# One queue of transfers, issued by GpSimd in place of SyncE, in a decode-attention forward and backward

## The chip, the cores and the metric

The kernel runs on one core of one Trainium2 chip. The metric is the device time of one execution in microseconds (us). Three runs of the kernel before took 645.79, 646.20 and 646.21 us; their median is 646.2 us.

The engines are named as the profile names them: PE is TensorE (PEld its weight loads), DVE is VectorE, ACT is ScalarE, POOL is GpSimd and SP is SyncE. A trailing q (SPq, POOLq) is the sequencer of an engine, which also issues transfers. The transfers themselves run on 16 DMA engines that the core has.

## The reference

One decode step of attention over 32 heads with one query row each, forward and all gradients:

```python
B, H, Sq, Skv, Dh = 1, 32, 1, 8192, 128          # all bf16
scores = jnp.einsum('bhqd,bhkd->bhqk', q, k) * scale
attn = softmax(scores, axis=-1)
out = jnp.einsum('bhqk,bhkd->bhqd', attn, v)
out, vjp = jax.vjp(forward, q, k, v)
return out, *vjp(grad_out)                        # out, dq, dk, dv
```

For one head, k and v are 8192 x 128 bf16 values, 2 MB each. The kernel must read both once (128 MB over the heads, in units of 2^20 bytes) and write dk and dv, which are as large. With p the softmax row, dv is the outer product of p and grad_out; dp = v grad_out; ds = p (dp - sum(p dp)) scale; dk is the outer product of ds and q; dq = ds k.

## The kernel before, in words

**Tiles.** A head's k (or v, dk, dv) lies in SBUF as one tile of 128 partitions by 64 rows by 128 values: partition p holds 64 successive rows, so each partition's share is one contiguous piece of 16 KB in memory. `Kt` has three buffers (`K_BUFS`), `Vt` two (`V_BUFS`), and the result tiles `G_dk` and `G_dv` two each.

**Transfers.** `load_k` (L74) and `load_v` (L78) load a head's tile with one transfer of 2 MB; only head 0's k comes in four chunks of 512 KB. `outer` (L225) stores a finished result tile with one transfer of 2 MB, or two of 1 MB for heads 0 and 31. `q` is loaded at L81 and `out` and `dq` are stored at L258, 8 KB each. All of these are issued by SP, in program order, on one queue. The one transfer that SP does not issue is the load of `grad_out`, which ACT issues. An issue waits on its engine's queue until its buffer is free (loads) or its data is there (stores), and holds up the issues behind it.

**Order of work.** The program first lists the q and grad_out loads, then `load_k(0)`, `load_v(0)`, `load_k(1)`, `load_v(1)`; after these stands `make_identity`, two POOL instructions that write `ident` (masks.py:197 and masks.py:199). From `tc.manual_schedule()` on, each engine executes in the order that the program is written in. POOL has nothing to do after `ident`.

`ident` is an input of nearly all of the opening: DVE's `in_quad` (L99), the four transposes of q (L111), `lane` (L113), `ident_f` (L115), and through these `q_blk` (L117). Only after `q_blk`, in DVE's order, come the block transposes of head 0's k (`k_blocks`, L146), and then PE's scores (L157).

The loop body for head h computes the scores of k (L157), the softmax (L163 to L311), the transposes of v (L188, with ACT's copies at L179), out (L205), dp (L200), and the four quarters of dv (L215); interleaved with it are the previous head's dq (L205) and the four quarters of dk (L215). `load_k(h + 2)` stands after dk's second quarter and `load_v(h + 2)` after dv's third, except in head 0, where `load_k(2)` has a free buffer at once.

Of the kernel before, what the change touches and what calls it, by code (L numbers as in the profile page):

```python
# [23 lines left out]
def kernel(  # L24
# [11 lines left out]
    nc = tc.nc  # L36
# [23 lines left out]
    Kt, Vt, XK, XV, st = {}, {}, {}, {}, {}  # L60

    def rows_of(x, h, c, parts):
        L = NT // parts
        return x[0, h].rearrange("(p n) d -> p n d", p=P)[:, c * L:(c + 1) * L, :]

    def slots(X, c, parts):
        L = NT // parts
        return X[:, c * L:(c + 1) * L, :]

    def load_k(h):  # L70
        Kt[h] = kpool.tile([P, NT, D], BF16, tag="K", name="Kt")
        parts = NCH if h == 0 else 1
        for c in range(parts):
            nc.sync.dma_start(slots(Kt[h], c, parts), rows_of(k, h, c, parts))  # L74

    def load_v(h):
        Vt[h] = vpool.tile([P, NT, D], BF16, tag="V", name="Vt")
        nc.sync.dma_start(Vt[h][:], rows_of(v, h, 0, 1))  # L78

    rows = consts.tile([H, 2, D], BF16)  # L80
    nc.sync.dma_start(rows[:, 0, :], q.rearrange("b h s d -> (b h s) d"))  # L81
    nc.scalar.dma_start(rows[:, 1, :], grad_out.rearrange("b h s d -> (b h s) d"))
    load_k(0)
    load_v(0)
    load_k(1)
    load_v(1)

    ident = consts.tile([P, P], BF16)
# [119 lines left out]
    def outer(h, which, r):  # L208
        x = st[h]
        if r == 0:  # L210
            x[which] = gpool.tile([P, NT, D], BF16, tag=which, name="G_" + which)
        G, dst = x[which], out_2 if which == "dk" else out_3
        rep, row = x["ds"] if which == "dk" else x["p"], x["qd"][:, 0 if which == "dk" else 1, :]
        Q = NT // 4
        nc.vector.tensor_tensor(  # L215
            slots(G, r, 4).rearrange("p n (a b) -> p n a b", b=R),
            slots(rep, r, 4).unsqueeze(2).to_broadcast([P, Q, D // R, R]),
            row.rearrange("p (a b) -> p a b", b=R).unsqueeze(1).to_broadcast([P, Q, D // R, R]),
            op=ALU.mult)
        parts = 1  # L220
        if h == 0 or h == H - 1:
            parts = 2
        if r % (4 // parts) == 4 // parts - 1:
            c = r // (4 // parts)
            nc.sync.dma_start(rows_of(dst, h, c, parts), slots(G, c, parts))  # L225

    def rows_bc(h):
        x = st[h]
# [22 lines left out]
    def result(src, dst):  # L251
        half = small.tile([P, H], BF16, tag="half", name="half")
        nc.scalar.copy(half[:], src[:])
        fin_ps = psT.tile([P, CH, P], BF16, tag="T", name="fin_ps")
        nc.tensor.transpose(fin_ps[0:H, 0, :], half[:], ident[:])
        fin_sb = small.tile([H, D], BF16, tag="fin", name="fin_sb")
        nc.scalar.copy(fin_sb[:], fin_ps[0:H, 0, :])
        nc.sync.dma_start(dst.rearrange("b h s d -> (b h s) d"), fin_sb[:])  # L258

    for h in range(H + 1):  # L260
        p_ = h - 1
# [8 lines left out]
        if h > 0:  # L270
            ds_of(p_)
            outer(p_, "dk", 0)
            dq_of(p_, 0)
# [3 lines left out]
        if h > 0:  # L277
            dq_of(p_, 1)
            outer(p_, "dk", 1)
        if 0 < h and h + 2 < H:  # L280
            load_k(h + 2)
# [7 lines left out]
        if h > 0:  # L289
            outer(p_, "dk", 2)  # L290
# [36 lines left out]
        if 0 < h and h + 2 < H:  # L327
            load_v(h + 2)
# [3 lines left out]
        if h == H - 1:  # L332
            result(o_all, out_0)

    result(dq_all, out_1)
    order.__exit__(None, None, None)

# [29 lines left out]
```

## Time and profile before

| what | value |
|---|---|
| median of three runs | 646.2 us |
| span of the profiled execution, first to last instruction | 644.6 us |
| bytes read and written | 134.23 MB and 134.23 MB |
| DMA engines busy with the SP queue (q1) | 98.2% of the span |
| DVE, PE, ACT, POOL busy | 78%, 75%, 28%, 0% |
| POOL instructions | 6 |

The profile gives the profiled execution's own time as its span only; the median of the runs is 1.6 us more than that span, which is taken here as what lies around it. Busy shares are averages over stages with different limits, so a stage is read by its own stretch of the trace. "DMA share" in a table of stretches is the mean busy share of the 16 DMA engines, GB/s what all of them moved. Beside the views, the trace holds a record for each DMA packet; where durations of packets are given, they are medians of these records.

### The profile page before, as it was taken

Reading aid. Unit: us, or ns where it says so; the run is one execution under the profiler, and the core shown is the slowest. Engines: PE = TensorE matmul, PEld = TensorE weight load, DVE = VectorE, ACT = ScalarE, POOL = GpSimd, SP = SyncE. Lnnn points to the kernel's source line nnn. Section 1 sums busy time; section 2 is a strip of 40 time slices with the busy share of each in tenths; the row PEclk is TensorE's granted clock in tenths of the full one; section 3 lists DMA queues with packets and bytes.
Section 4 is the critical chain, followed back from the end, with each engine's and each line's share of the span. In section 5 each row is a group of like instructions: output and inputs, shape, how many; then the busy total and the mean of one; then the engine's idle time right before and its main releaser. Section 6 shows DMA issues by size and latency. Waiting matters only on the chain.

```text
span 644.6 us, 20935 instructions
## 1 busy us (share of the span) xinstructions
PE 482.0 (75%) x9673; PEld 443.9 (69%) x9673; DVE 505.9 (78%) x653; ACT 180.7 (28%) x332; POOL 0.7 (0%) x6
## 2 busy tenths in 40 slices
PE   3998898886777877768776787677876777877780
PEld 2887788785676766768666687567776676866670
DVE  5999899767977679867788777787767986778761
ACT  2333333322233231333222332123322233231230
POOL 0000000000000000000000000000000000000000
PEclk9666666665566655666556665566665566655665
DMA  8999999999999999999999999999999999999985
GB/s 350 404 428 429 424 427 424 428 429 421 418 429 428 428 425 430 430 426 431 425 428 428 430 426 428 428 428 427 427 429 431 424 432 424 430 426 429 427 362 244
DMA packets 19718, 269.80 MB, mean 419 GB/s; under 512 B 2352, under 2 KB 2352, under 8 KB 2864
## 3 DMA queue, kind: packets, MB, share of 16 engines
q1 hardware_dynamic: 19584, 268.47, 98.2%
q8 instruction: 75, 1.23, 0.7%
q14 instruction: 11, 0.09, 0.0%
q10 hardware_dynamic: 48, 0.01, 0.0%
HBM read 134.23 MB, written 134.23 MB: 416 GB/s over the span
## 4 chain that ended last, share of the span: by engine, by line
DMA 62%; PE 24%; DVE 9%; ACT 1%; issue 1%; SPq 0%; DVEq 0%; ACTq 0%
DMA Vt<-in_v_dram 61%; PE T_ps L188 15%; DVE XK_sb L146 4%; DVE G_dv L215 4%; PE m_ps L205 3%; PE dp_ps L200 2%; PE s_ps L157 2%; PE dp_ps L205 1%; DVE G_dk L215 1%; DMA Kt<-in_k_dram 1%; PE m_ps L300 1%; ACT p_rep L309 0%; PE s_ps L173 0%; ACT XT_sb L179 0%; PE m_ps L288 0%
## 5 line engine op out<-in xcount | busy, mean ns | idle before, releaser
L188 PE MATMUL T_ps<-ident_f,Vt 128*128 128x128 f32 x1024 | 217.0, 383 | 27.3 <-DMA Vt<-in_v_dram 24.7
L188 PEld LDWEIGHTS T_ps<-ident_f,Vt 128*128 128x128 f32 x1024 | 182.2, 206 | 45.2 <-PE m_ps L288 21.7
L215 DVE TENSOR_TENSOR G_dv<-p_rep,qd 128x2048 bf16<-128x2048 bf16 x128 | 148.2, 1220 | 60.9 <-DMA out_dram<-G_dv 52.8
L215 DVE TENSOR_TENSOR G_dk<-ds_rep,qd 128x2048 bf16<-128x2048 bf16 x128 | 155.6, 1218 | 4.6 <-DMA out_dram<-G_dk 3.6
L146 DVE STREAM_TRANSPOSE XK_sb<-Kt 128x1024 f32<-128x1024 f32 x128 | 148.3, 1214 | 5.8 <-DMA Kt<-in_k_dram 3.2
L179 ACT COPY XT_sb<-T_ps 128x1024 f32<-128x1024 f32 x128 | 128.7, 1008 | 83.9 <-PE T_ps L188 77.2
L157 PE MATMUL s_ps<-q_blk,XK_sb 128*128 128x4 bf16 x2048 | 59.8, 168 | 94.6 <-DVE pdt L239 87.6
L157 PEld LDWEIGHTS <-XK_sb 128*128 128x128 bf16 x2048 | 57.1, 104 | 103.9 <-DVE pdt L239 96.6
L200 PE MATMUL dp_ps<-do_blk,XT_sb 128*128 128x2 bf16 x2048 | 67.0, 164 | 18.0 <-ACT XT_sb L179 17.6
L200 PEld LDWEIGHTS <-XT_sb 128*128 128x128 bf16 x2048 | 65.5, 103 | 20.7 <-ACT XT_sb L179 20.2
L205 PE MATMUL dp_ps<-ds_rep,Kt 128*128 128x1 bf16 x2048 | 64.0, 165 | 0.4 <-DVE ds_rep L241 0.4
L205 PEld LDWEIGHTS <-Kt 128*128 128x128 bf16 x2048 | 59.5, 104 | 5.7 <-issue 5.6
L249 ACT COPY dq_all<-dp_ps 128x1 f32<-128x1 f32 x32 | 5.1, 159 | 205.2 <-PE dp_ps L205 182.8
L205 PEld LDWEIGHTS <-Vt 128*128 128x128 bf16 x2048 | 57.0, 96 | 0.7
L205 PE MATMUL m_ps<-p_rep,Vt 128*128 128x1 bf16 x2048 | 56.5, 163 | 0.0
L309 ACT ACTIVATE p_rep<-e,rinv 128x256 bf16<-128x256 f32 x32 | 16.3, 508 | 64.6 <-DVE rinv L307 64.6
L307 DVE RECIPROCAL rinv<-m_ps 128x1 f32<-128x1 f32 x32 | 5.4, 168 | 35.2 <-PE m_ps L300 35.1
L234 ACT CAST qd<-s_ps 128x256 bf16<-128x256 f32 x32 | 11.9, 372 | 32.5 <-PE s_ps L230 32.5
L299 ACT ACTIVATE e<-s_ps,nbias 128x64 f32<-128x64 f32 x32 | 10.1, 314 | 32.5 <-DVE nbias L295 32.5
L241 DVE SCALAR_TENSOR_TENSOR ds_rep<-dp_ps,pdt,p_s 128x256 bf16<-128x256 f32 x32 | 15.5, 484 | 4.6 <-PE dp_ps L200 1.3
L163 DVE TENSOR_TENSOR sm<-s_ps,in_quad 128x256 f32<-128x256 f32 x32 | 13.6, 425 | 6.0 <-PE s_ps L157 2.0
L300 PEld LDWEIGHTS m_ps<-rs,ones_f 128*128 128x128 f32 x64 | 17.6, 334 | 0.0
(44 smaller groups left out, 153.1 us busy)
## 6 DMA issues: line engine op xcount, KB each, us to landing
Vt<-in_v_dram SPq DMA_DIRECT2D x32, 2048.0 KB, 30.1
Kt<-in_k_dram SPq DMA_DIRECT2D x31, 2048.0 KB, 30.3
out_dram<-G_dv SPq DMA_DIRECT2D x30, 2048.0 KB, 34.5
out_dram<-G_dk SPq DMA_DIRECT2D x30, 2048.0 KB, 33.7
out_dram<-G_dv SPq DMA_DIRECT2D x4, 1024.0 KB, 14.4
out_dram<-G_dk SPq DMA_DIRECT2D x4, 1024.0 KB, 13.2
Kt<-in_k_dram SPq DMA_DIRECT2D x4, 512.0 KB, 5.1
out_dram<-fin_sb SPq DMA_DIRECT2D x2, 8.0 KB, 12.8
```

What stands on the lines that cost most here:

```text
L146: nc.vector.transpose(XK[h][:, :, :, u, :], slots(Kt[h], u, NCH).rearrange("p g d -> p (g d)").bitcast(F32).rearrange("p (g w j) -> p g w ...
L157: nc.tensor.matmul(out[:, g, :], lhsT=cols[:, g, c // 2, c % 2], rhs=q_blk[:, h, c, :], start=(c == 0), stop=(c == 2 * NB - 1), skip_group ...
L163: nc.vector.tensor_tensor(x["sm"][:], x["s"][:, 0:NT].rearrange("p (a g) -> p a g", a=NQ).unsqueeze(2) .to_broadcast([P, NQ, NCH, CH]), in ...
L179: nc.scalar.copy(X[:], st[h].pop("T")[:])
L188: nc.tensor.transpose(T_ps[:, i, :], words[:, m * P:(m + 1) * P], ident_f[:])
L200: nc.tensor.matmul(st[h]["dp"][:, n:n + 2], lhsT=X[:, i, e2, :], rhs=do_blk[:, h, e2, :], start=(e2 == 0), stop=(e2 == 1), skip_group_chec ...
L205: nc.tensor.matmul(out_col, lhsT=Xt[:, n, :], rhs=rep[:, n, 0:1], start=(n == 0), stop=(n == NT - 1), skip_group_check=True)
L215: nc.vector.tensor_tensor(slots(G, r, 4).rearrange("p n (a b) -> p n a b", b=R), slots(rep, r, 4).unsqueeze(2).to_broadcast([P, Q, D // R, ...
L234: nc.scalar.copy(x["qd"][:].rearrange("p a d -> p (a d)"), x["s"][:, 256:512])
L241: nc.vector.scalar_tensor_tensor(out=x["ds"][:], in0=x["dp"][:, 0:NT].unsqueeze(2).to_broadcast([P, NT, R]), scalar=pdt[:], in1=x["p_s"][: ...
L300: nc.tensor.matmul(x["m"][:, 0:1], lhsT=ones_f[:], rhs=rs[:], start=True, stop=True, skip_group_check=True)
L309: nc.scalar.activation(x["p"][:], e[:].unsqueeze(2).to_broadcast([P, NT, R]), ACT.Copy, scale=rinv[:])
```

## The change

All transfers that SP issued are issued by POOL. The order in which they are written, their sizes and the number of queues stay. ACT still issues the load of grad_out. Five issue sites change, which give 138 transfers: 35 loads of k (four of them the chunks of head 0), 32 loads of v, 68 stores of dk and dv, and three of 8 KB (q, out, dq).

```diff
@@ def load_k(h):
-            nc.sync.dma_start(slots(Kt[h], c, parts), rows_of(k, h, c, parts))
+            nc.gpsimd.dma_start(slots(Kt[h], c, parts), rows_of(k, h, c, parts))
@@ def load_v(h):
-        nc.sync.dma_start(Vt[h][:], rows_of(v, h, 0, 1))
+        nc.gpsimd.dma_start(Vt[h][:], rows_of(v, h, 0, 1))
@@ load of q
-    nc.sync.dma_start(rows[:, 0, :], q.rearrange("b h s d -> (b h s) d"))
+    nc.gpsimd.dma_start(rows[:, 0, :], q.rearrange("b h s d -> (b h s) d"))
     nc.scalar.dma_start(rows[:, 1, :], grad_out.rearrange("b h s d -> (b h s) d"))
     load_k(0)
     load_v(0)
@@ def outer(h, which, r):
-            nc.sync.dma_start(rows_of(dst, h, c, parts), slots(G, c, parts))
+            nc.gpsimd.dma_start(rows_of(dst, h, c, parts), slots(G, c, parts))
@@ def result(src, dst):
-        nc.sync.dma_start(dst.rearrange("b h s d -> (b h s) d"), fin_sb[:])
+        nc.gpsimd.dma_start(dst.rearrange("b h s d -> (b h s) d"), fin_sb[:])
```

## The prediction

> **What bounds the kernel now.** I read the page first, then stretches of the trace, the opening in order of time, and the issues with their times to landing. From the page come the transfer load, the queue's share and the chain that ended last:
>
> ```profile
> DMA  8999999999999999999999999999999999999985
> GB/s 350 404 428 429 424 427 424 428 429 421 418 429 428 428 425 430 430 426 431 425 428 428 430 426 428 428 428 427 427 429 431 424 432 424 430 426 429 427 362 244
> ...
> q1 hardware_dynamic: 19584, 268.47, 98.2%
> ...
> DMA 62%; PE 24%; DVE 9%; ACT 1%; issue 1%; SPq 0%; DVEq 0%; ACTq 0%
> ...
> Vt<-in_v_dram SPq DMA_DIRECT2D x32, 2048.0 KB, 30.1
> Kt<-in_k_dram SPq DMA_DIRECT2D x31, 2048.0 KB, 30.3
> ```
>
> All slices but the first and the last stand at 9, and the chain is 62% transfer. A load of 2 MB takes 2.097 MB / 427 GB/s = 4.9 us of the 16 DMA engines, but lands 30.3 us after its issue: some 25 us of other transfers stand ahead of it. SP issues far ahead of need, so a later issue is free until it eats those 25 us.
>
> The stretches show how level the middle is and what the end looks like (columns: busy time of PE, PEld, DVE, ACT, POOL, granted clock, DMA share, GB/s):
>
> ```profile
> 100.00:560.00 460.00, 349.23 (x6962) 320.81 (x6961) 362.85 (x463) 129.71 (x233) 0.00 (x0) 0.59 1.01 427
> ...
> 632.00:634.00 2.00, 0.00 (x0) 0.00 (x0) 0.00 (x0) 0.00 (x0) 0.00 (x0) 0.50 0.96 401
> 634.00:636.00 2.00, 0.00 (x0) 0.00 (x0) 0.00 (x0) 0.00 (x0) 0.00 (x0) 0.50 0.58 241
> ...
> 638.00:640.00 2.00, 0.00 (x0) 0.00 (x0) 0.00 (x0) 0.00 (x0) 0.00 (x0) 0.50 0.57 242
> ```
>
> In the middle no DMA engine idles. At the end 0.57 of 16, that is nine engines, still work for 6 us and more after the other seven are done. The nine late ones set the end.
>
> How far compute could run without transfers is in the chain in order of time (start, us, what):
>
> ```profile
> 17.09 4.63 DVE G_dv L215 x4
> ...
> 84.34 4.63 DVE G_dv L215 x4
> ...
> 135.42 1.94 PE T_ps L188 x8
> ...
> 614.30 1.94 PE T_ps L188 x8
> ```
>
> Four heads take 84.34 - 17.09 = 67.3 us while compute leads: 16.8 us each. Once transfers lead, 24 heads take 614.30 - 135.42 = 478.9 us: 19.95 us each. The margin is 3.1 us per head.
>
> **The change part by part.** It adds and removes no byte; 138 issues leave SP and go to POOL, which has only six instructions (0.7 us busy). Nothing is queued on SP after them. Five costs follow, (a) being the price of one issue.
>
> *(a) One issue.* SP's rows give 0.33 us for a store and 0.39 to 0.46 us at the opening. POOL issues nothing in this trace. Bounds: below, SP's 0.33 us; above, 1.5 us, the whole of the smallest transfer (q, 8 KB, from issue to landing), since making a list of 128 rows should not exceed making one of 32, moving it and reporting it. I take 1.1 us, which is q's 1.5 us less its 0.39 us of issue: POOL must do in instructions what a unit does for SP, so I lean to the upper row.
>
> *(b) The first transfer.* The opening, in order of time:
>
> ```profile
> 0.73 0.20 POOL masks.py:197 MEMSET ident<- 128x128 bf16 x1 [0.29 <-POOLq L351]
> 0.74 0.39 SPq L81 DMA_DIRECT2D rows<-in_q_dram  x1
> ...
> 1.01 0.29 POOL masks.py:199 TENSOR_SCALAR_AFFINE_SELECT ident<-ident 128x128 bf16<-128x128 bf16 x1
> 1.19 1.84 SPq L74 DMA_DIRECT2D Kt<-in_k_dram  x4
> ...
> 3.26 0.86 DVE L117 TENSOR_TENSOR q_blk<-tp_q,in_quad 128x128 bf16<-128x128 bf16 x4
> ...
> 7.85 2.47 DVE L146 STREAM_TRANSPOSE XK_sb<-Kt 128x1024 f32<-128x1024 f32 x2 [0.40 <-DMA Kt<-in_k_dram]
> ```
>
> q's issue and the first of four K chunks end at 1.19 + 1.84/4 = 1.6 us; packets follow. With two POOL issues from 0.73 us it is 0.73 + 2 x 1.1 = 2.9 us: +1.3 us. Nothing covers that, since from here on the DMA engines never idle. The other three chunks come 1.1 us apart and each needs 0.524 MB / 427 GB/s = 1.23 us, so they keep up. At 0.33 us per issue the term is -0.2 us; at 1.5 us it is +2.1 us, plus 3 x 0.27 us for the chunks, +2.9 us.
>
> *(c) `ident` behind the loads.* In program order eight issues (q, four chunks, v0, k1, v1) stand ahead of `make_identity` on POOL. `ident` is ready at 0.73 + 8 x 1.1 + 0.5 = 10.0 us, not 1.3. Behind it are `in_quad` 0.29, `four` 0.62, transposes 0.6, `q_blk` 0.86 and four block transposes of 1.23 each: 17.3 us in place of 10.3, so compute is 7 us late. The cover is what the queue holds:
>
> ```profile
> Kt<-in_k_dram SPq DMA_DIRECT2D x1, 2048.0 KB, 26.3
> ...
> out_dram<-G_dv SPq DMA_DIRECT2D x1, 1024.0 KB, 14.3
> ```
>
> The first line is k2, issued at 4.79 us: it lands at 31.1 us. The second is head 0's first dv half, issued at 19.48 us, far before that. After the change it would be ready at 19.48 + 7 = 26.5, issued by 27.6, against a queue that drains at 31.1 + 1.3 = 32.4 us: hidden by 4.8 us. The second half (21.8 + 7 + 1.1 = 29.9 against 34.9) and v2 (23.4 + 7 + 1.1 = 31.5 against 37.3) are hidden too. At 1.5 us per issue compute is 10.2 us late, the first half is issued by 31.2 against 34.0 us: still hidden. Cost zero; if the cover were gone, each us beyond it would cost one. Slack per head then returns the 7 us, 3.1 us at a time.
>
> *(d) The other 130 issues.* Each is up to 0.8 us longer, hidden behind 25 us of queue. In the tail, the last dk half is issued after 630.4 us and the late engines run until 643 us; that half is 8 packets of 0.31 us (packet records) on each engine, 2.5 us, so 10 us of slack hide 2 x 1.1 us. Zero.
>
> *(e) The packets.* The records show per DMA engine 611 ns for 16 KB, 309 ns for 8 KB, 159 ns for 4 KB, and one packet of 4 bytes, 9 ns, that closes each transfer. If POOL's lists have the same packets the cost is zero. One more closing packet per transfer would be 138 x 9 ns = 1.2 us. Below zero nothing is likely: the 16 KB packet already runs 26.8 GB/s in every slice. I take half of it, 0.6 us.
>
> Sum: +1.3 + 0 + 0 + 0.6 = +1.9 us on a span of 644.6 us; with the 1.6 us around it, 648.1 us. The median before is 646.2 us. A difference under 0.2% (1.3 us) is about what a measurement of this kernel cannot tell from none.
>
> Two rules stand against the rows. DVE is busy 78% of the span, its longest runs being four G_dv products and four block transposes, 4.63 + 4.5 = 9.2 us; the 25 us of queue cover even a list that waits for all of that. The Trainium skill's page "SBUF — State Buffer" (the note on DVE blocking a DMA issued from GpSimd) says that GpSimd can't write its descriptors while certain VectorE instructions hold the shared port pair, and advises SyncE or ScalarE; no row here shows POOL issuing. By it alone, with the queue as cover, the sum does not change. The page "DMA: Bandwidth & Descriptors", Specifications, gives about 1 us to the first byte for a GpSimd transfer and 0.6 us from SyncE. As an estimate worked out from that page, (b) would be 0.4 us in place of 1.3, and the whole 647.2 us.
>
> **The rivals.**
>
> *Transfers run slower.* POOL's lists could cut the 16 KB rows, or load some engines more than others. For it: 15,744 packets of 16 KB make up nearly all the time, and nothing here shows POOL's packets. Against it: sizes in the code are unchanged. Cut at 8 KB: 15,744/16 x (2 x 309 - 611) ns = 984 x 7 ns = 6.9 us, so 655 us; at 4 KB, 984 x 25 ns = 24.6 us, 673 us.
>
> *DVE is held up by POOL's writing.* It decides from 3.1/4 = 0.78 us of DVE time lost per issue, four issues a head. At 0.9 us, 0.12 x 4 x 32 = 15 us: 663 us. For it: compute would become the bound with only 16% to spare. Against it: DVE has idle time before its G_dv products (60.9 us in all) that takes up part.
>
> *Nothing shows.* An issue costs 0.6 us or less, or `ident` is written first: 646 to 647 us. For it: SP's issue is 0.33 us and the queue hides almost everything.
>
> *Faster.* The nine late engines run over 6 us longer than the seven. If POOL's lists share rows out so that this is evened, the nine give up 7/16 of some 7 us to 9 us of lag: 3 to 4 us, 643 to 644 us. For it: the seven are idle at the end. Against it: all transfers have 128 rows, a multiple of 16, so a share other than eight each has no reason.
>
> **How the numbers follow.** Chances: the forecast's case 47, of which 13 lie within 0.2% (under 647.5 us); slower transfers 20; DVE held up 6; nothing shows 17, of which 2 end below -0.2%; faster 10. Slower 34 + 20 + 6 = 60, same 13 + 15 = 28, faster 12. The likeliest case alone spans 646.0 us (-0.2 in (b), 0 in (e)) to 650.3 us (+2.9 and +1.2). The range goes down to 644.0, the dearer half of the faster case, and up to 661.0, past the 8 KB cut (655 us) and a third of the way on to the 4 KB cut (673 us); it leaves out about 5 below and 13 above.
>
> **What would show it.** (a) SPq's issue rows turn into POOLq rows; the gap between successive chunks at the opening gives the price. (b) First K data moves from about 2.2 to 3.5 us. (c) `in_quad` starts near 10 us, L146 ends near 17 us, and the DMA share stays at 9 from 20 to 45 us; a dip there would be cover that failed. (d) Loads still land about 30 us after issue. (e) 19,584 packets in the data queue and 427 GB/s in the middle; more packets, or fewer GB/s, mean the slower-transfer rival. If heads stay 19.95 us apart, only the opening counts; DVE's mean time of 1.22 us for G_dv rising above 1.3 us would mean that DVE is held. The prediction is wrong if an issue on POOL takes several us, or if the middle's rate moves at all: 1% of it is 6 us.

## The result and the profile after

The changed kernel takes 648.05 us (median of five runs, 647.40 to 648.86) against 646.15 us for the kernel before beside it: a ratio of 1.0032, with a 95% interval of 1.0019 to 1.0044. The forecast was 648.1 us, slower. That the number was met so closely is luck: the two terms that it put above zero were both too large, and another one, of 1.0 us, was missing.

The page of the changed kernel, with the lines that answer to those of before:

```profile
DMA  8999999999999999999999999999999999999985
GB/s 321 409 425 430 422 424 426 428 425 428 430 428 426 429 428 427 427 427 431 428 424 429 432 423 432 426 430 421 425 432 424 429 429 427 423 430 427 426 359 228
...
q0 software_dynamic: 19536, 268.47, 97.9%
...
Vt<-in_v_dram POOLq DMA_DIRECT2D x32, 2048.0 KB, 29.4
Kt<-in_k_dram POOLq DMA_DIRECT2D x31, 2048.0 KB, 29.9
```

The same bytes move on another queue at the same rate. Loads still land 29 to 30 us after their issue, so POOL too issues some 25 us ahead. The middle, in the same stretch as before (columns as there; POOL is the fifth, 49.86 us):

```profile
100.00:560.00 460.00, 350.96 (x6980) 322.94 (x6978) 364.81 (x466) 129.78 (x236) 49.86 (x94) 0.59 1.01 427
```

427 GB/s at a DMA share of 1.01, as before. Where, then, are the 1.7 us of span (646.3 less 644.6)? The opening, in order of time:

```profile
1.28 0.64 POOL L81 DMA_DIRECT2D rows<-in_q_dram  x1 [0.83 <-POOLq L351]
1.91 2.13 POOL L74 DMA_DIRECT2D Kt<-in_k_dram  x4
...
5.59 0.22 POOL masks.py:197 MEMSET ident<- 128x128 bf16 x1
5.74 0.53 POOL L74 DMA_DIRECT2D Kt<-in_k_dram  x1
6.36 0.30 POOL masks.py:199 TENSOR_SCALAR_AFFINE_SELECT ident<-ident 128x128 bf16<-128x128 bf16 x1
...
8.63 4.60 DVE L146 STREAM_TRANSPOSE XK_sb<-Kt 128x1024 f32<-128x1024 f32 x4
```

One issue takes 0.53 us on POOL (the first, q's, 0.64), and q's starts at 1.28 us, where SP's stood at 0.74. By the packet records the first packet of k starts at 3.17 us instead of 2.22. `ident` is complete at 6.7 us, and L146 ends at 13.2 instead of 10.3 us.

The end shows in SP's waits at the last line of the program, first in the kernel before and then in the changed kernel (waiting line, what it waits for, us in total, times, longest):

```profile
SPq L362 <- PEq L362: 0.6, 2, 0.4
```

```profile
SPq L362 <- PEq L362: 1.6, 2, 1.2
```

SP waits 1.0 us longer for the other engines after its last transfer has landed. The instructions of that line say for whom (changed kernel; durations min/median/max in ns, first and last start in us):

```profile
L362 POOLq DRAIN  x3: 46/87/13567, 632.0 to 646.0; - x3
L362 SPq DRAIN  x3: 7/7/7, 644.5 to 645.8; - x3
```

POOL's long drain starts at 632.0 us, behind its last issue, and ends at 632.0 + 13.57 = 645.6 us. SP had passed its own waits at 644.5. In the kernel before, no POOL drain is longer than 0.39 us:

```profile
L362 POOLq DRAIN  x3: 34/78/389, 1.0 to 644.3; - x3
```

With the packet records the span splits without a rest. "Stretch" runs from the first to the last data packet, "end" from there to the last instruction:

| kernel | first data packet | stretch | end | span |
|---|---|---|---|---|
| before | 2.22 | 640.82 | 1.57 | 644.6 |
| changed | 3.17 | 640.54 | 2.57 | 646.3 |
| difference | +0.95 | -0.28 | +1.00 | +1.7 |

These are two single executions. The medians differ by 1.9 us, which is what the first packet and the end add up to (0.95 + 1.00). The -0.28 of the stretch is less than executions of one kernel differ by: the eleven of the run with the tail on SP, for example, have spans from 644.5 to 646.1 us. The end too varies by itself: it is 1.4 to 1.9 us in the kernel before and in the six runs below in which POOL does not finish last.

### The profile page after: what moved, and what is told of

It reads as the page before. It is cut to its first block, busy times and chain, and to the rows that moved or that the text cites. A ratio compares the mean times of both kernels' runs of the same rounds, so it can differ in the third digit from the quotient of the medians.

```text
span 646.3 us, 20936 instructions
## 1 busy us (share of the span) xinstructions
PE 481.8 (75%) x9673; PEld 444.0 (69%) x9673; DVE 505.4 (78%) x653; ACT 180.4 (28%) x332; POOL 73.9 (11%) x144
## 4 chain that ended last, share of the span: by engine, by line
issue 69%; DMA 14%; POOL 9%; DVE 4%; PE 1%; POOLq 0%; ACT 0%; DVEq 0%; ACTq 0%
DMA Kt<-in_k_dram 9%; DMA Vt<-in_v_dram 5%; POOL out_dram L225 4%; POOL Kt L74 2%; DVE XK_sb L146 2%; POOL Vt L78 2%; PE s_ps L157 1%; DVE G_dv L215 1%; DVE G_dk L215 1%; PE T_ps L188 0%; DVE sm L163 0%; POOLq L225 0%; DVE q_blk L117 0%; POOL rows L81 0%; DVE mx L284 0%
## 5 line engine op out<-in xcount | busy, mean ns | idle before, releaser
L215 DVE TENSOR_TENSOR G_dv<-p_rep,qd 128x2048 bf16<-128x2048 bf16 x128 | 148.2, 1221 | 59.2 <-DMA out_dram<-G_dv 48.7
L146 DVE STREAM_TRANSPOSE XK_sb<-Kt 128x1024 f32<-128x1024 f32 x128 | 147.9, 1213 | 4.7 <-DMA Kt<-in_k_dram 2.0
L74 POOL DMA_DIRECT2D Kt<-in_k_dram x35 | 18.6, 533 | 219.2 <-PE dp_ps L205 219.2
L78 POOL DMA_DIRECT2D Vt<-in_v_dram x32 | 17.0, 532 | 215.5 <-PE m_ps L320 215.5
L225 POOL DMA_DIRECT2D out_dram<-G_dk x34 | 18.1, 532 | 84.8 <-DVE G_dk L215 65.6
L225 POOL DMA_DIRECT2D out_dram<-G_dv x34 | 18.1, 532 | 36.5 <-DVE G_dv L215 31.5
## 6 DMA issues: line engine op xcount, KB each, us to landing
out_dram<-G_dv POOLq DMA_DIRECT2D x4, 1024.0 KB, 13.2
```

Source lines behind the costliest of these rows:

```text
L74: nc.gpsimd.dma_start(slots(Kt[h], c, parts), rows_of(k, h, c, parts))
L78: nc.gpsimd.dma_start(Vt[h][:], rows_of(v, h, 0, 1))
L146: nc.vector.transpose(XK[h][:, :, :, u, :], slots(Kt[h], u, NCH).rearrange("p g d -> p (g d)").bitcast(F32).rearrange("p (g w j) -> p g w ...
L215: nc.vector.tensor_tensor(slots(G, r, 4).rearrange("p n (a b) -> p n a b", b=R), slots(rep, r, 4).unsqueeze(2).to_broadcast([P, Q, D // R, ...
L225: nc.gpsimd.dma_start(rows_of(dst, h, c, parts), slots(G, c, parts))
```

## The experiments

Theory A: the cost sits at the two ends, 0.95 us before the first packet and 1.0 us in POOL's drain, and the middle is free. Theory B: `ident` behind the loads, which made compute 2.9 us late, is the cost. Theory C: POOL's issues or packets cost a little each in the middle. Spans and packets below come from one profiled execution of a run, times are medians with the ratio to the kernel before on the same chip. The kernel before is at 645.8 to 646.0 us on those chips, so sums that start from 646.15 us can be 0.2 to 0.4 us high.

### Opening back on SP

```diff
+ (nc.sync if h <= 2 else nc.gpsimd).dma_start(... k ...)
+ (nc.sync if h <= 1 else nc.gpsimd).dma_start(... v ...)
+ nc.sync.dma_start(... q ...)
```

> Only the opening goes back to SP: q, k0 (four chunks), v0, k1, v1 and k2; the other 128 transfers stay on POOL, ident is written at once. Theory A (the ends: a first packet 0.95 us later and a drain of POOL's list that ends about 1.0 us after SP's own waits would; the middle is free): span 646.3 - 0.95 = 645.3 us, time 647.1 us, and POOL's last drain still ends some 1.9 us after the last data packet. Theory B (ident behind the loads, which made compute 2.9 us late, is the whole cost): span 644.6 us, time 646.2 us. Theory C (the middle: POOL's issues or packets cost a little each): span 646.3 us, time 648.0 us.

Measured 647.41 us (1.0022, 1.0006 to 1.0037), span 645.9. The first data packet is back at 2.21 us and the end stays long at 2.27 us, as A says, and B is refuted: with `ident` written at once the time does not return to that of the kernel before. (Its interval, 646.3 to 648.3 us, holds both A's and C's time.) But the stretch is 641.44 us, 0.9 longer than in the changed kernel, which A does not explain. The packet records say where it is: this execution's data packets took 633.2 us per DMA engine, against 631.7 in the changed kernel and in the kernel before. (The run had 129 transfers on POOL, not 128.)

### Tail back on SP

```diff
+ (nc.sync if h == H - 1 else nc.gpsimd).dma_start(... dk, dv ...)
+ nc.sync.dma_start(... out, dq ...)
```

> Only the tail goes back to SP: head 31's stores of dv and dk and the two 8 KB stores; the opening and the middle stay on POOL. Theory A: POOL's drain is over before the last data lands, so span 646.3 - 1.0 = 645.3 us, time 647.05 us, with the first data packet still at 3.2 us. Theory B and theory C: span 646.3 us, time 648.0 us.

Measured 647.05 us (1.0019, 1.0010 to 1.0028), span 644.8. First data packet 3.17, end 1.41 us. A's time exactly; the interval (646.6 to 647.8 us) leaves out B's and C's 648.0. The drain is off the path when POOL's last transfers land before SP's:

```profile
L362 POOLq DRAIN  x3: 46/103/23625, 615.7 to 644.5; - x3
L362 SPq DRAIN  x3: 7/7/7, 644.0 to 644.3; - x3
```

It ends at 615.7 + 23.6 = 639.3 us, and SP is ready only at 644.0.

### Opening and tail back on SP

> Opening and tail both go back to SP, the 122 transfers between stay on POOL. Theory A: span 644.3 to 644.6 us, time 646.0 to 646.2 us, as before the change. Theory B: the same 644.6 us (the opening alone does it, as in the run with the opening on SP). Theory C: span 646.2 us or more, time 647.9 us.

Measured 646.90 us (1.0015, 1.0006 to 1.0024). Both ends are as in the kernel before (2.23 and 1.42 us), but the stretch is 642.44 us and the median 0.8 us above A. The two ends are confirmed, and the middle is not quite free here, although it was in the run with the tail alone (stretch 640.25 us). The profiled execution was the slowest of the eleven. Its packets took 633.0 us per engine, which is 1.3 of the 1.6 us that its stretch is above the kernel before. What lifts the median is not shown by one trace.

### `ident` first

```diff
+ ident = consts.tile([P, P], BF16)
+ make_identity(nc, ident[:])
  rows = consts.tile([H, 2, D], BF16)
  nc.gpsimd.dma_start(... q ...)
```

> All on POOL as in the change, but the two instructions that write ident stand ahead of the first k chunk on POOL. Compute is ready some 3 us sooner, the first k packet 0.3 to 0.5 us later. Theory A: span 646.6 to 646.8 us, time 648.3 to 648.5 us, although compute starts earlier. Theory B: span 644.9 us, time 646.5 us. Theory C: span 646.3 us, time 648.0 us.

Measured 648.29 us (1.0045, 1.0032 to 1.0058), span 646.5. L146 ends at 11.6 instead of 13.2 us, so compute starts 1.6 us sooner, and the first data packet comes at 3.54 us, 0.37 later. The span follows the packet (+0.2 us), not the compute. This is A against B in one run: making POOL's useful work earlier made nothing faster, since it put two instructions ahead of the first load. The times of this run and the changed kernel's overlap; the verdict rests on the order of events, not on their difference.

### Opening alone, and tail alone, on POOL

The same two parts from the other side, on the kernel before.

> The kernel before, with only the opening moved to POOL: q, k0 (four chunks), v0, k1, v1, k2; the other 128 transfers stay on SP. Theory A (two ends, middle free): first data packet at 3.2 us in place of 2.2; time from the last data packet to the end as before, 1.6 us; span 644.6 + 0.95 = 645.6 us, time 647.1 us. Theory B (late ident is the whole cost): span 646.3 us, time 648.0 us. Theory C (a little per transfer in the middle): span 644.6 to 644.8 us, time 646.2 us.

Measured 647.11 us (1.0024, 1.0015 to 1.0033) against A's 647.1; first data packet 3.15 us, stretch 640.06 us. It is 1.26 us above the kernel before, a little more than the 0.93 us by which the packet is later. This run matters for a rival that the first three leave open: by their times alone, a middle that costs 1 us on POOL, with ends that cost less, would do as well. Here the middle is on SP, and the opening alone costs its full price. The changed kernel's own stretch, no longer than before, says the same.

> The kernel before, with only the tail moved to POOL: head 31's stores of dv and dk and the two 8 KB stores. Theory A: first data packet at 2.2 us, and the end comes 2.3 to 2.6 us after the last data packet in place of 1.6; span 645.5 us, time 647.0 us. If that drain grows with the number of transfers that POOL has issued (6 here, 138 in the change), it stays at 1.6 us and the span at 644.6 us. Theory B and C: span 644.6 us, time 646.2 us.

Measured 646.26 us (1.0007, 0.9999 to 1.0016), first data packet 2.22, end 1.82 us, and SP's last wait 0.6 us as before. With six transfers on POOL the drain (630.7 + 12.75 = 643.4 us) is over before SP's own waits are (643.6). So the drain is not a fixed price; the expectation's second case holds. Two more runs went to what sets it.

### What the drain grows with

```diff
+ (nc.gpsimd if h >= 16 else nc.sync).dma_start(... k, v, dk, dv ...)   # tail on POOL; h >= 7 in the second run
```

> The second half of all heads on POOL, with the tail: about 68 transfers on POOL, opening and first half on SP. If POOL's last drain takes longer the more transfers POOL has issued (SP's last wait for the other engines was 0.6 us with 6 transfers on POOL, 1.2 with 129, 1.6 with 138): that wait 0.8 to 1.0 us, span 644.9 us, time 646.5 us. If the count does not matter: 0.6 us, 644.6 us, 646.1 us, or 1.6 us, 645.6 us, 647.1 us. Rival D as above adds 0.8 us to any of these.

> Heads 7 to 31 and the tail on POOL, the first seven heads on SP: 104 transfers on POOL, fewer than the 138 of the change. Theory E (POOL's last drain takes 0.55 us plus 0.042 us for each transfer that it has not retired yet, from 0.8 us with 6 and 3.4 us with 68; the 138 and 129 transfers that took only 1.8 and 1.5 us had some 108 retired on the way): the drain ends 4.9 us after the last packet, span 648 to 650 us, time 650 to 652 us, longer than with all 138 on POOL. If the drain's length has another cause than the count: 1.5 to 3.4 us after the last packet, span 645.5 to 648 us, time 647 to 649.7 us.

The drains, first with 68 and then with 104 transfers on POOL:

```profile
L362 POOLq DRAIN  x3: 40/102/16475, 630.9 to 647.9; - x3
L362 SPq DRAIN  x3: 7/7/7, 644.9 to 647.6; - x3
```

```profile
L362 POOLq DRAIN  x3: 40/102/16727, 630.8 to 648.0; - x3
L362 SPq DRAIN  x3: 7/7/7, 643.8 to 647.8; - x3
```

SP is ready at 644.9 and 643.8 us and the drains end at 647.4 and 647.5. The times are 649.88 us (1.0058, 1.0044 to 1.0072) and 650.35 us (1.0067, 1.0049 to 1.0085): with half of the transfers on POOL the kernel is slower than with all of them. The first of the two was not foreseen (at most 647.9 us with every surcharge), and its drain gave the rule for the second, which was: 4.9 us predicted, 4.9 measured. From the end of POOL's last packet to the end of its drain, in all runs with transfers on POOL:

| transfers on POOL | 6 | 9 | 62 | 68 | 70 | 104 | 123 | 129 | 132 | 138 |
|---|---|---|---|---|---|---|---|---|---|---|
| us | 0.8 | 0.8 | 3.1 | 3.4 | 3.5 | 4.9 | 1.1 | 1.5 | 1.4 | 1.8 |

(9, 62 and 70 are the runs with the opening on POOL, with half the middle and with all stores on POOL; the three with 138 agree within 0.03 us.) From 6 to 104 it is 4.13 us for 98 transfers, 0.042 us each. From 123 to 138 it rises at about the same pace (0.7 us for 15) from a base lower by some 108 transfers. The reading that fits is that POOL retires landed transfers one at a time and does so once on the way, whatever is left being paid at the end. The trace of the changed kernel shows a pause where this would be, ahead of the 115th issue:

```profile
513.97 0.53 POOL L74 DMA_DIRECT2D Kt<-in_k_dram  x1 [7.88 <-PE dp_ps L205]
518.86 0.54 POOL L225 DMA_DIRECT2D out_dram<-G_dk  x1 [4.36 <-issue]
```

POOL stands for 4.36 us and waits for nothing that the profile shows; at 0.042 us this is some 104 transfers. All six runs with 123 or more transfers have one such pause, ahead of the 114th or 115th issue (4.3 to 4.4 us, and 2.6 us in the run with zeros below). The runs with 104 or fewer have none. So the retiring on the way is seen. That a full list triggers it is only argued, and so is the count as such: nearly all transfers here have the same number of packets, so transfers and packets are not told apart.

### Two queues with work at once

The opening-and-tail run left 0.8 us open. Handing over from SP's queue to POOL's was the suspect.

```diff
+ (nc.gpsimd if h >= 16 else nc.sync).dma_start(... k, v ...)
+ (nc.gpsimd if 16 <= h < H - 1 else nc.sync).dma_start(... dk, dv ...)   # opening, first half, tail on SP
```

> Only the second half of the middle on POOL: k, v, dk and dv transfers of heads 16 to 31, without head 31's stores and the two 8 KB stores; opening, first half and tail on SP. Theory A (the middle is free): first data packet 2.2 us, wait for the other engines at the end 0.6 us as in the kernel before, span 644.6 us, time 646.1 us. Rival D (handing over from SP's queue to POOL's costs something by itself, which would explain why opening and tail together on SP measured 646.9 and not 646.1 us): span 645.4 us or more, time 646.9 us.

Measured 647.69 us (1.0025, 1.0014 to 1.0036), 1.7 us above the kernel before: this handing over costs. At the handover, SP's load of v15 (issued at 263.8 us) lands 40.9 us later and its next store of dk after 44.4 us, while POOL's loads of k16 and v16, issued 10 and 21 us after v15's, land after 15.7 and 15.0 us. The newcomer overtakes what the other queue holds. The rate stays at 427 GB/s and the stretch is 641.33 us, in the fastest of the nine executions. The packet records place the loss at the end: from 630 us to the last packet the 16 DMA engines together stand idle for 92 us, against 77 in the kernel before. That is 1.0 us per engine; ahead of 630 us their idle time is the same. The run with 68 transfers hands over at the same head and has 91 us (stretch 641.66 us). But the run with 104 transfers hands over too, at head 7, its k7 overtakes in the same way (15.3 us to landing beside 41.7 for a store of SP), and it has 71 us and a stretch of 640.32 us. So overtaking alone is not the price. Why the engines finish further apart after one handover and not after the other is open.

A run that keeps both queues busy throughout shows the effect enlarged:

```diff
  nc.sync.dma_start(... q, k, v ...)          # all loads on SP
  nc.gpsimd.dma_start(... dk, dv, out, dq ...) # all stores on POOL
```

> All loads on SP, all stores on POOL (70 transfers), so both queues work side by side throughout. Theory E: drain ends 3.5 us after the last packet, 2.7 us more at the end than on SP alone; with a free middle span 647.2 us, time 648.9 us. Rival D (two queues with work at once cost by themselves): 1 to 2 us or more on top, and the rate in the middle falls or the engines finish further apart. If two queues help: the rate in the middle rises above 427 GB/s and the span falls below 644 us.

Measured 657.6 us (1.0178, 1.0163 to 1.0194). The drain took the 3.5 us that were predicted for 70 transfers. The rest is in the GB/s by slices, and in the landings:

```profile
GB/s 348 416 425 428 427 428 425 429 426 428 428 428 429 428 425 428 428 428 425 427 428 427 429 427 429 428 427 426 417 426 421 414 428 421 421 423 419 359 291 145
...
Vt<-in_v_dram SPq DMA_DIRECT2D x32, 2048.0 KB, 24.0
Kt<-in_k_dram SPq DMA_DIRECT2D x31, 2048.0 KB, 23.3
out_dram<-G_dv POOLq DMA_DIRECT2D x30, 2048.0 KB, 35.4
out_dram<-G_dk POOLq DMA_DIRECT2D x30, 2048.0 KB, 34.4
```

The rate until slice 28 is the same. Loads now land 11 us sooner than stores, so they run ahead of them, and the last three slices (359, 291, 145) are worse than in the kernel before (427, 362, 244). There the transfers run out for a while (this run first, then the kernel before):

```profile
625.00:629.00 4.00, 4.00 (x41) 4.00 (x39) 3.56 (x9) 1.36 (x5) 0.53 (x1) 0.50 0.08 29
```

```profile
625.00:629.00 4.00, 2.53 (x73) 2.15 (x70) 3.75 (x4) 0.89 (x4) 0.00 (x0) 0.50 0.82 341
```

The last load is issued at 594.6 us instead of 583.2 and the last large store at 642.1 instead of 630.4. The loads and the stores issued so far are done before the next results are there, and the DMA engines stand nearly idle for 4 us (share 0.08, against 0.82). Slower packets, most of them after 460 us, add 2.1 us per engine. What makes compute late was not followed further. Two queues move nothing faster here, and they undo the order that one queue keeps.

### How deep the cover is

Here POOL fills each later buffer with zeros between its wait and the load's issue; the load overwrites them.

```diff
+        if h > 2:
+            nc.gpsimd.memset(Kt[h][:], 0.0)
         nc.gpsimd.dma_start(... k ...)
+        if h > 1:
+            nc.gpsimd.memset(Vt[h][:], 0.0)
         nc.gpsimd.dma_start(... v ...)
```

> The change, with POOL also writing zeros into the whole buffer of each later load (k from head 3 on, v from head 2 on) before it issues that load: by the 0.20 us of ident's 128 x 128 fill some 6.7 us of POOL work between the wait and the issue, 59 times. Theory A (a queue 25 us deep covers the issue, order unchanged): the rate in the middle stays 427 GB/s, span 646 to 648 us, time 648 to 650 us; loads land some 7 us sooner after their issue, that is about 23 us. Theory C, or any theory in which the time of an issue is on the path: 59 x 6.7 us = up to 395 us more; at a tenth of that still 40 us.

Measured 653.22 us (1.0118, 1.0104 to 1.0132). The fills take 6.93 us each, 59 of them 409 us, and all but 5 us of that vanishes. The page:

```profile
GB/s 322 409 348 386 423 428 427 426 428 425 430 426 429 428 429 428 426 428 431 427 428 427 424 432 429 427 429 427 428 428 427 425 427 429 423 427 426 427 378 205
...
Vt<-in_v_dram POOLq DMA_DIRECT2D x32, 2048.0 KB, 22.3
Kt<-in_k_dram POOLq DMA_DIRECT2D x31, 2048.0 KB, 22.9
```

Loads land 7 us sooner after their issue, because the issue is 7 us later and the landing is not. Only slices 3 and 4 lose rate. The stretches there:

```profile
30.00:40.00 10.00, 10.00 (x176) 9.40 (x173) 9.70 (x14) 3.74 (x7) 9.70 (x4) 0.53 1.00 356
40.00:50.00 10.00, 8.45 (x247) 7.88 (x244) 9.69 (x17) 1.96 (x5) 9.41 (x5) 0.64 0.96 346
50.00:60.00 10.00, 9.41 (x148) 9.07 (x146) 9.87 (x12) 4.91 (x8) 9.70 (x6) 0.67 1.00 383
```

(427 - 356 + 427 - 346 + 427 - 383) GB/s over 10 us each are 1.96 MB, or 4.6 us of transfers: nearly the whole 5.0 us by which the stretch grows (645.50 against 640.54). From 20 to 60 us loads of the changed kernel land 15.5 us after their issue, not 30; there the cover was thin. Yet the DMA engines were not short of work for long (DMA share 1.00, 0.96 and 1.00). Their packets took longer: one of 16 KB has a mean of 765 ns from 34 to 60 us, against 619 in the changed kernel, and over the whole run the data packets take 635.8 us per engine instead of 631.7, that is 4.1 of the 5.0 us. What lengthens packets while the queue is shallow is not shown. C is refuted in the large: what an issue costs is free while the queue is deep. While it was shallow, the four fills that began before 58 us (27.7 us) cost 5.0 us, a fifth or so of their time.

### K first

If a shift of the first packet goes through whole, the kernel before has 0.45 us to gain: SP issues q ahead of k.

```diff
-    nc.sync.dma_start(rows[:, 0, :], q.rearrange("b h s d -> (b h s) d"))
+    nc.scalar.dma_start(rows[:, 0, :], q.rearrange("b h s d -> (b h s) d"))
```

> The kernel before, all transfers on SP, only the load of q issued by ACT, ahead of grad_out's: SP's first issue is then k0's first chunk. Theory A (a shift of the first packet goes through to the end whole): first data packet at 1.8 us in place of 2.2, span 644.15 us, time 645.7 us, 0.45 us below the kernel before. Theory B: q lands later or not, compute is not earlier, span 644.6 us, time 646.2 us.

Measured 645.49 us against 645.85 us (0.9994, 0.9985 to 1.0002); first data packet at 1.74 us, span 644.0. The shift is there. That this kernel is faster than the one before is likely but not settled by the interval.

## Why the prediction was right, and where it was not

**(a) The price of an issue** was taken as 1.1 us and is 0.53 us back to back. Of the two bounds, SP's 0.33 and q's whole 1.5 us, the lower was the nearer. The lean to the upper row was the mistake.

**(b) The first transfer** was to be 1.3 us later and is 0.95. The parts: q's issue starts 0.54 us later (1.28 against 0.74), which was not foreseen; k's first issue then starts 0.63 instead of 0.45 us behind it, +0.18; from there to the first packet it is 1.26 instead of 1.03 us, +0.23. That nothing covers this term was right: the runs with only the opening on POOL and with only the tail on SP are 1.3 and 1.1 us above the kernel before. The run with only the opening on SP gives back 0.6 us; in its profiled execution slower packets hide the rest.

**(c) `ident` behind the loads**: compute was to be 7 us late and is 2.9 us late, as (a) halves. That it would be hidden was right, and the run with `ident` first shows that it is.

**(d) The middle and the tail** were both set to zero. The middle holds while there is one queue: the changed kernel's stretch is 640.54 us in an execution at its median time. In the tail the last issues are hidden as said, but the step looked only at issues and packets. POOL's drain, 1.0 us on the path, was not among the costs or the rivals. This is the step that failed. The kernel before shows a POOL drain of at most 0.39 us, with no transfer behind it, so a bound for it should have been set and was not.

**(e) The packets** were given 0.6 us for half a closing packet per transfer. The records show 2,208 packets of 4 bytes, as before, and 48 fewer in all: the three transfers of 8 KB go as 16 packets of 512 bytes each instead of 32 of 256. (The prediction's "all transfers have 128 rows" overlooks these three, which have 32.) The cost is zero.

So 1.3 + 0.6 = 1.9 us were predicted, and 0.95 + 1.0 - 0.28 = 1.7 us of span came. Two terms were too large by 0.35 and 0.6 us, the drain's 1.0 us was missing, and they cancelled by luck.

Of the rivals, slower transfers did not occur: a 16 KB packet takes 611 ns on either queue. DVE was not held up by the issues: `G_dv` takes 1,221 ns on average (before 1,220), and the issues were not held up by DVE, since the 34 of `G_dv` range from 531 to 562 ns though DVE is busy 78% of the time (88 of its products and block transposes overlap an issue). The rule that the prediction took from the Trainium skill's page "SBUF — State Buffer" (the note on DVE blocking a DMA) therefore did not bite here; this kernel's long VectorE work is products of two inputs and block transposes. The page "DMA: Bandwidth & Descriptors", Specifications, gives 0.4 us more to the first byte for GpSimd. From the start of the first k issue to its first packet it is 1.03 us on SP (1.19 to 2.22) and 1.26 us on POOL (1.91 to 3.17), 0.23 us more; the other 0.72 us of the 0.95 are q's issue and its late start.

## What to carry to other kernels

In a kernel that is bound by one deep queue of transfers, as this one is, ask of a change to the issuing engine three things first: when the first packet starts, how deep the queue is where it is shallowest, and what the issuing engine must still do after the last packet. The price of an issue in between could grow by 7 us here and cost nothing once the queue was 25 us deep. And test a forecast by its terms: this one's total was right to 0.1 us while both terms that it put above zero were off and another was missing.

## What the runs showed of the hardware

- POOL's final drain takes 0.8 us after its last packet with 6 transfers and 0.042 us more for each further one up to 104; with 123 to 138 it is short again (1.1 to 1.8 us), and those runs have a pause of POOL of up to 4.4 us ahead of the 114th or 115th issue. With 68 and 104 transfers on POOL, the last ones among them, the kernel was slower (649.9 and 650.4 us) than with all 138 (648.05).
- Two queues with work share the DMA engines, so a transfer that is issued later on the emptier queue lands first: 15 to 16 against 41 to 44 us at a handover, with the rate unchanged at 427 GB/s.
- While POOL fills a buffer (6.93 us), one kind of DVE instruction stands still. `p_s` (L311, L315 in that run), a product of a 128 x 64 tile with scalars, takes 254 to 256 ns in the changed kernel; the second line is beside the fills:

```profile
L311 DVE TENSOR_SCALAR p_s<-e,rinv x32: 254/255/256, 19.4 to 617.5; 128x64 f32<-128x64 f32 x32
L315 DVE TENSOR_SCALAR p_s<-e,rinv x32: 253/3450/5821, 19.4 to 621.0; 128x64 f32<-128x64 f32 x32
```

  Its longest is 5.8 us. Of its 32, the 29 that meet a fill all end 0.04 to 0.06 us behind the end of that fill; the other three take 253 to 256 ns. The block transposes (1,212 ns) and `G_dk` (1,217 ns) are untouched; `G_dv`, which follows `p_s`, has a mean of 1,472 ns at a busy time of 150 us (148 in the changed kernel), so its records overlap the held instruction. The Trainium skill's page "SBUF — State Buffer" has the rule under "Who interferes with whom": whichever of such a VectorE instruction and a GpSimd instruction starts first blocks the other. This run agrees for a fill; POOL's issues of transfers had no such effect: in the changed kernel five of the 32 overlap an issue and take 254 to 256 ns.
- Some 16 KB packets take up to 1.8 us instead of 0.611, in bursts at places that differ from run to run (near 160 us in the kernel before, near 180 us with the opening on SP). The data packets take 631.7 us per DMA engine in the kernel before and 633.2 us in that run, so the bursts are part of the spread of about 1 us between executions, and are why differences below that rest here on the order of events.
